# A decode attention block: two opening loads moved ahead of the start barrier

## The chip, the cores and the metric

One core of one Trainium2 chip (trn2). The metric is the device time of the whole program in microseconds, lower is better. The span in a profile runs from the first recorded instruction to the last, and is shorter than the time of the same run.

## The reference, cut to what matters

One decoding step for four sequences: layernorm, attention over a cache of 8192 positions, and a small gated MLP branch on the same input.

```python
def reference(A_x, A_k_cache, A_v_cache, A_wq, A_wo, B_x, B_w1, B_w2, B_w3, B_w4):
    # B=4, D=448, Hq=16, Hkv=8, Sk=8192, Dh=256, F=1792; all bf16
    x = A_x
    xn = _layernorm(x, axis=-1)
    s = _A_ref(xn, A_k_cache, A_v_cache, A_wq, A_wo)      # q = xn@wq; softmax(q k^T) v; @wo
    g = _silu(_B_ref(xn, B_w1, B_w2, B_w3, B_w4))         # only w3, w4 matter for Sq=1
    return x + s * g
```

K and V are 4 x 8 heads of 4 MiB each: 64 loads of 4 MiB, 268 of the 279 MB that the kernel reads.

## The kernel before

SyncE's program issues every large load in the order in which the stream is to run. ScalarE issues one small one, x (4 rows of 896 bytes). `begin_ahead` takes these first loads out of their programs and puts them behind the Drain with which their engine arrives at the program's opening barrier.

```python
def begin_ahead(nc, loads):
    # ... takes the loads out of their blocks ...
    first = blocks[0].instructions
    for load in reversed(loads):
        at = next(n for n, i in enumerate(first)
                  if i.engine == load.engine and isinstance(i, mybir.InstDrain))
        first.insert(at + 1, load)
```

```python
        def prog_sp(sp):
            ahead.append(sp.sem_inc(S["pause"], 1))          # two steps that let x go first
            ahead.append(take(sp, "pause"))
            ahead.append(sp.dma_start(vflat[1][:, 0:DK * HDH], ... A_wq ...).then_inc(S["dwq"], 16))
            sp.dma_start(... B_w3 ...).then_inc(S["dw3"], 16)
            sp.dma_start(... B_w4 ...).then_inc(S["dw4"], 16)

            def load_k(h):
                b, g = where(h)
                if h >= 2:
                    sp.wait_ge(S["v_k"], h - 1)              # buffer of head h-2 free
                sp.dma_start(kn_dst(h), A_k_cache[b, g]...).then_inc(S["dk%d" % (h % 2)], 16)
            # ... load_v waits for v_v in the same way ...
            load_k(0)
            load_k(1)
            load_wo(NLATE, HQ, "dwo")                        # 2688 KB
            for h in range(2, NH):
                load_k(h)
                load_v(h - 2)
            load_v(NH - 2)
            load_v(NH - 1)
            # ... LATE pieces of wo, 448 and two times 224 KB, then the store ...
```

```python
        def prog_act(act):
            ahead.append(act.dma_start(x_sb[:, :], x2d).then_inc(S["dx"], 16))
            # ...
        def prog_dve(v):
            # ...
            c(v.memset(q_ps[:, 0:QW], 0.0))
            v.wait_ge(S["dx"], 16)
            c(v.tensor_copy(x_f[:, :], x_sb[:, :]))          # "the cast": the front chain begins
            # ... layernorms, then with PE: q, h, gelu, h2, the gate ...
            # ... per head: evacuations of the K transposes, then
                    v.sem_inc(S["v_k"], 1)                   # lets SyncE issue K of head h+2
        def prog_pe(pe, xn_mark, xn2_mark):
            # ... front chain: transposes, q, h, h2, hs ...
            for i in range(NWARM):                           # NWARM = 14 warming matmuls
                pe.matmul(psv[0:PVW, 0:QW], pT[:, 0, 0:PVW], wq_sb[:, 0, 0:QW], start=True, stop=True)
            # ... then per head: f_t, 128 transposes of K in 16 groups, waits for the K load ...
```

The K buffer has two slots. So the third K load, called K2 below, is the first load that waits for computed work: for VectorE's last evacuation of head 0, which needs the whole front chain and the warming matmuls done.

## Time and profile before

| | before |
|---|---|
| median of the runs, us | 653.56 (653.2 to 653.56, 3 runs) |
| profiled run, us / its span, us | 653.45 / 652.0 |
| first wq packet, us into the span | 1.26 |
| last wo piece landed, us into the span | 649.13 |
| tail from there to the end, us | 2.87 |
| outside the span, us | 1.45 |

The prediction below shows and reads the page, the stretches and the opening. Two things are added here. First the start of head 0 on PE (timeline of the kernel before: start us, length us, engine, line, operation; L596 are the warming matmuls, L604 the transposes of K):

```profile
23.94 5.26 PE L596 MATMUL psv<-vb,pT 128*32 128x512 bf16 x14
30.07 1.05 PE L604 MATMUL pst<-ident_b,kn 128*128 128x128 bf16 x16 [0.87 <-PEq L278]
```

Second SyncE's issue of K2, from its timeline:

```profile
41.77 0.33 SPq L237 DMA_DIRECT2D kn<-in_A_k_cache_dram  x1
```

The load ahead of K2 in the stream is the large piece of wo; its 16 engines land it between 44.35 and 46.24.

### The profile page before, as it was taken

How to read it: one execution, taken by the hardware profiler on the slowest of the kernel's cores; microseconds unless marked ns; L12 is line 12 of the kernel's file. 1: busy time of each engine (PE TensorE's matmuls, PEld its weight loads, DVE VectorE, ACT ScalarE, POOL GpSimd, SP SyncE). 2: the span in 40 equal slices, each digit the busy share in tenths (PEclk: the TensorE clock that was granted, in tenths of full speed). 3: DMA queues.
4: the chain of work that ended last, by engine and by line, in shares of the span. 5: the costliest groups of instructions: out<-in, count | busy, mean ns of one | idle time of the engine just before them, and what ended most of it. 6: DMA issues, size and time to landing. Idle time of an engine off the chain costs nothing. (4 is left out here: it accounts for less than half of the span.)

```text
span 652.0 us, 22813 instructions
## 1 busy us (share of the span) xinstructions
PE 550.5 (84%) x9937; PEld 470.7 (72%) x9937; DVE 276.9 (42%) x622; ACT 255.8 (39%) x364; POOL 3.6 (1%) x17
## 2 busy tenths in 40 slices
PE   2799997988887987888897888898888798878897
PEld 1487876987676876667787766787677688757774
DVE  7344544343343443434443444444344344434442
ACT  4144543443343443323443333444234344423440
POOL 2000000000000000000000000000000000000000
PEclk9998999888799898889987888988779987978999
DMA  9999999999999999999999999999999999999997
GB/s 374 440 420 433 430 434 434 430 438 426 440 426 440 426 440 426 440 428 436 432 435 430 434 434 426 440 426 440 426 440 428 438 428 438 430 436 430 434 429 301
DMA packets 12353, 279.13 MB, mean 428 GB/s; under 512 B 1204, under 2 KB 3256, under 8 KB 3768
## 3 DMA queue, kind: packets, MB, share of 16 engines
q1 hardware_dynamic: 12328, 278.99, 99.5%
q8 instruction: 7, 0.11, 0.1%
q10 hardware_dynamic: 16, 0.01, 0.0%
q14 instruction: 2, 0.02, 0.0%
HBM read 278.99 MB, written 0.00 MB: 428 GB/s over the span
## 5 line engine op out<-in xcount | busy, mean ns | idle before, releaser
L604 PE MATMUL pst<-ident_b,kn 128*128 128x128 bf16 x4096 | 342.7, 237 | 81.4 <-PEq L278 79.3
L309 ACT ACTIVATE kT<-pst 128x1024 bf16<-128x1024 bf16 x224 | 229.3, 1024 | 357.5 <-ACTq L278 356.3
L604 PEld LDWEIGHTS pst<-ident_b,kn 128*128 128x128 bf16 x4096 | 271.7, 107 | 87.2 <-issue 86.6
L307 DVE COPY kT<-pst 128x1024 bf16<-128x1024 bf16 x288 | 197.5, 691 | 261.1 <-DVEq L278 261.1
L616 PE MATMUL psc<-qc,kT 128*128 128x2 bf16 x4096 | 178.2, 164 | 0.0
L616 PEld LDWEIGHTS psc<-qc,kT 128*128 128x128 bf16 x4096 | 157.1, 98 | 28.7 <-issue 28.5
L655 PE MATMUL psv<-vb,pT 128*4 128x512 bf16 x1056 | 85.6, 378 | 0.0
L634 PE MATMUL psm<-sel,po 128*128 128x2 f32 x272 | 36.8, 257 | 0.5 <-PEq L278 0.5
L634 PEld LDWEIGHTS psm<-sel,po 128*128 128x128 f32 x272 | 34.8, 196 | 0.9 <-issue 0.9
L655 PEld LDWEIGHTS psv<-vb,pT 128*4 128x4 bf16 x1056 | 21.8, 82 | 15.0 <-issue 0.4
L466 DVE TENSOR_REDUCE rmax<-psc 128x2 f32<-128x128 f32 x32 | 9.3, 292 | 48.1 <-DVEq L278 48.1
L484 DVE COPY po<-psv 128x512 f32<-128x512 f32 x34 | 23.5, 691 | 4.0 <-DVEq L278 3.3
L331 ACT ACTIVATE pT<-psc,negb 128x64 bf16<-128x64 f32 x66 | 20.6, 332 | 5.4 <-ACTq L278 5.4
L471 DVE TENSOR_REDUCE gmax<-psm 2x1 f32<-2x128 f32 x32 | 8.9, 279 | 32.3 <-DVEq L278 32.3
L628 PEld LDWEIGHTS psm<-diag,ones_f 2*128 2x128 f32 x66 | 13.5, 253 | 6.3 <-issue 5.0
L628 PE MATMUL psm<-diag,ones_f 2*128 2x2 f32 x66 | 16.2, 313 | 1.1 <-PEq L278 0.9
L331 ACT ACTIVATION_READ_ACCUMULATOR pT<-psc,negb 128x1 f32 x66 | 13.6, 206 | 0.0
L624 PEld LDWEIGHTS psm<-ident_f,rmax 128*2 128x2 f32 x32 | 2.6, 80 | 14.0 <-issue 14.0
L646 PE MATMUL psm<-rowsum,ones_f 128*128 128x2 f32 x64 | 11.6, 251 | 0.0
L552 PE MATMUL pst<-ident_b,xn_b 4*128 4x4 bf16 x14 | 0.6, 161 | 11.5 <-DVE xn_b L379 6.8
L646 PEld LDWEIGHTS psm<-rowsum,ones_f 128*128 128x128 f32 x64 | 9.5, 188 | 0.0
L474 DVE TENSOR_SCALAR diag<-ident_f,gmax 2x2 f32<-2x2 f32 x32 | 6.9, 217 | 4.8 <-DVEq L278 1.1
(101 smaller groups left out, 101.1 us busy)
## 6 DMA issues: line engine op xcount, KB each, us to landing
kn<-in_A_k_cache_dram SPq DMA_DIRECT2D x32, 4096.0 KB, 25.5
vb<-in_A_v_cache_dram SPq DMA_DIRECT2D x31, 4096.0 KB, 30.5
vb<-in_A_wq_dram SPq DMA_DIRECT2D x1, 3584.0 KB, 11.4
vb<-in_B_w_dram SPq DMA_DIRECT2D x2, 1568.0 KB, 16.3
wo_sb<-in_A_wo_dram SPq DMA_DIRECT2D x1, 2688.0 KB, 43.3
kn<-in_A_v_cache_dram SPq DMA_DIRECT2D x1, 2048.0 KB, 24.7
kn<-in_A_v_cache_dram SPq DMA_DIRECT2D x1, 1024.0 KB, 26.7
kn<-in_A_v_cache_dram SPq DMA_DIRECT2D x2, 512.0 KB, 27.9
```

Of the source, the lines that this page charges most:

```text
L307: engine.tensor_copy(dst, src).then_inc(S["v_ev"], 1)
L309: engine.activation(dst, src, ACT.Copy).then_inc(S["a_ev"], 1)
L331: ins = act.activation(pv_p[:, :, hh], sc[:, :, hh], ACT.Exp, bias=negb[:, s, hh:hh + 1], scale=SCALE, accum_out=rowsum[:, s, hh:hh + 1])
L466: v.tensor_reduce(rmax[:, :], psc[h % 2][:, 0:NCH * REP].rearrange("p (k h) -> p h k", h=REP), AX.X, ALU.max).then_inc(S["v_rmax"], 1)
L471: v.tensor_reduce(gmax[:, :], psm[0:REP, 0:P], AX.X, ALU.max).then_inc(S["v_s"], 1)
L484: v.tensor_copy(po[:, slot], psv[:, 0:CP * DH]).then_inc(S["v_po"], 1)
L604: ins = pe.transpose(dst[:, t * P:(t + 1) * P], kn[:, h % 2, GC * j + kl, half * P:(half + 1) * P], ident_b[:, :])
L616: ins = pe.matmul(psc[h % 2][:, kk * REP:(kk + 1) * REP], kT[:, j % RING, t * P:(t + 1) * P], qc[:, h % 2, half, :], start=(half == 0), st ...
L628: pe.matmul(psm[:, P:P + REP], ones_f[0:REP, :], diag[:, :], start=True, stop=True).then_inc(S["p_m2"], 1)
L634: ins = pe.matmul(dst(dh)[:, 0:width], po[:, slot, i * DH + dh:(i + 1) * DH:NHALF], sel[:, i, 0:width], start=(i == 0), stop=(i == CP - 1))
L646: pe.matmul(psm[:, P + REP:P + 2 * REP], ones_f[:, :], rowsum[:, h % 2, :], start=True, stop=True)
L655: ins = pe.matmul(psv[o:o + CP * REP, 0:CP * DH], pT[:, h % 2, kk * REP:(kk + CP) * REP], src[:, kk:kk + CP, :].rearrange("p c d -> p (c d)"),
```

## The change

The intent: start the stream earlier. wq is to be the first thing that SyncE does, ahead of its arrival at the barrier, and the two pause steps that kept x first are dropped; in exchange x is to go ahead of ScalarE's arrival.

```diff
-    first = blocks[0].instructions
-    for load in reversed(loads):
-        at = next(n for n, i in enumerate(first)
-                  if i.engine == load.engine and isinstance(i, mybir.InstDrain))
-        first.insert(at + 1, load)
+    first = list(blocks[0].instructions)
+    for n, load in enumerate(loads):
+        own = [i for i in first if i.engine == load.engine]
+        drain = next(i for i in own if isinstance(i, mybir.InstDrain))
+        if n == 0:
+            later = own[0:2]
+            first = [i for i in first if i not in later]
+            at = first.index(drain)
+            first[at:at] = later
+            at = first.index(later[0])
+        else:
+            at = first.index(drain)
+        first.insert(at, load)
     blocks[0].instructions = first
 ...
         def prog_sp(sp):
-            ahead.append(sp.sem_inc(S["pause"], 1))
-            ahead.append(take(sp, "pause"))
-            ahead.append(sp.dma_start(
+            ahead.insert(1, sp.dma_start(
                 vflat[1][:, 0:DK * HDH], ... A_wq ...).then_inc(S["dwq"], 16))
 ...
         def prog_act(act):
-            ahead.append(act.dma_start(x_sb[:, :], x2d).then_inc(S["dx"], 16))
+            ahead.insert(0, act.dma_start(x_sb[:, :], x2d).then_inc(S["dx"], 16))
```

Loop bodies, tiles, loads and their order are the same.

More of the change, by code (lines that the diff above doesn't have):

```diff
@@ L182, in bass_recurrent_scan__gqa_block_cached__mixer_s_mlp__decode_kernel @@
         S = {n: es.enter_context(nc.semaphore(n)) for n in (
-            ["dx", "dwq", "dw3", "dw4", "dwo", "dk0", "dk1", "dv0", "dv1", "dout", "pause"]
+            ["dx", "dwq", "dw3", "dw4", "dwo", "dk0", "dk1", "dv0", "dv1", "dout"]
             + ["dvl%d" % i for i in range(NPIECE)] + ["dwl%d" % i for i in range(len(LATE))]
```

## The prediction

> **What bounds the kernel now.** I read the page first: busy shares, the 40 slices, the DMA queues, the chain that ended last. Then the landings of the loads, the queue's own waits, and last the first 12 us as a timeline, because the change touches nothing else. From the page:
>
> ```profile
> span 652.0 us, 22813 instructions
> ...
> PE 550.5 (84%) x9937; PEld 470.7 (72%) x9937; DVE 276.9 (42%) x622; ACT 255.8 (39%) x364; POOL 3.6 (1%) x17
> ...
> DMA  9999999999999999999999999999999999999997
> GB/s 374 440 420 433 430 434 434 430 438 426 440 426 440 426 440 426 440 428 436 432 435 430 434 434 426 440 426 440 426 440 428 438 428 438 430 436 430 434 429 301
> ...
> q1 hardware_dynamic: 12328, 278.99, 99.5%
> ```
>
> The reader is to see one queue, SyncE's, that keeps the 16 DMA engines busy 99.5% of the span and moves 278.99 MB. No slice but the first and the last falls under 420 GB/s. PE at 84% has slack. The kernel is one unbroken stream of loads with a lead-in and a tail. The same cut by stretches (us, then busy time of PE, PEld, DVE, ACT and POOL, granted clock, DMA share, GB/s):
>
> ```profile
> 0.00:0.50 0.50, 0.00 (x0) 0.00 (x0) 0.00 (x0) 0.00 (x0) 0.20 (x4) 1.00 0.00 0
> 0.50:1.00 0.50, 0.00 (x0) 0.00 (x0) 0.08 (x1) 0.11 (x1) 0.27 (x2) 1.00 0.00 0
> ...
> 44.35:645.00 600.65, 517.66 (x9454) 447.91 (x9448) 251.74 (x536) 239.49 (x345) 0.00 (x0) 0.90 1.00 433
> ...
> 649.13:652.00 2.87, 0.55 (x8) 0.23 (x4) 0.77 (x2) 0.00 (x0) 0.00 (x0) 1.00 0.01 4
> ```
>
> Nothing moves in the first microsecond; then the stream runs at 433 GB/s; the last piece of wo lands at 649.13 and 2.87 us of output work follow. Packets in flight, counted from the trace's packet records, stay near the 16 engines from 1.55 us to 647 us without a hole. So
>
> time = start of the first wq packet (1.26 us) + stream (to 649.13) + tail (2.87) + 1.5 outside the span (653.45 for the profiled run less 652.0).
>
> Only something that shifts the first term, or tears a hole into the second, moves the result. The opening, from the timeline (start us, length us, engine, line):
>
> ```profile
> 0.21 0.56 ACTq L312 DMA_DIRECT2D x_sb<-in_A_x_dram  x1
> ...
> 0.24 0.41 SPq L222 DMA_DIRECT2D vb<-in_A_wq_dram  x1
> ...
> 0.73 0.20 POOL L284 MEMSET ident_f<- 128x128 f32 x1 [0.29 <-POOLq L816]
> 0.78 0.34 SPq L226 DMA_DIRECT2D vb<-in_B_w_dram  x1
> ...
> 0.92 0.48 DVE L383 MEMSET pst<- 128x512 f32 x1 [0.92 <-ACTq L816]
> ...
> 2.01 0.38 DVE L385 CAST x_f<-x_sb 4x448 f32<-4x448 bf16 x1 [0.60 <-DMA x_sb<-in_A_x_dram]
> ```
>
> Both loads leave 0.2 us into the span already, before the barrier opens. What lies ahead of wq is in the trace's records of SyncE, which the views leave out as not busy: Drain (its arrival at the barrier) at 0.000, the pause increment at 0.069, the pause wait at 0.149, wq at 0.237. ScalarE has its Drain at 0.133 and x at 0.207. TensorE arrives last, at 0.322; GpSimd sees the fourth arrival at 0.532, opens at 0.610, and SyncE passes at 0.695.
>
> **What the Trainium skill says.** "DMA: Bandwidth & Descriptors", Where 436 GB/s comes from, puts the ceiling of the fabric at 435.2 GB/s. The trace agrees: 433 GB/s over 600 us, and each 4 MiB load lands 9.68 us after the one before (4194304 B / 9.68 us = 433 GB/s). So no packing helps; only the start can. The same page, Issuing engines are not separate DMA queues, says loads issued from different engines run on the same 16 DMA engines. "Perfetto Trace Analysis", DMA Instruction — HWDGE, says that an issue locks a shared descriptor generator for exclusive use; before's x and wq issues overlap (0.21 to 0.77, 0.24 to 0.65), which neither shows nor refutes it. "DMA: Bandwidth & Descriptors", Queues, rings and completion order, says each DMA engine takes turns between its rings at packet granularity. Before's x packets start at 1.156 to 1.610 and wq's from 1.257 on, so x was mostly first and the trace does not show a small load queued behind wq.
>
> **The change, part by part.**
>
> 1. Pause steps gone, and wq ahead of SyncE's Drain. The three SyncE steps ahead of wq took 0.237 us together. wq becomes the first instruction of SyncE's program, so its issue moves from 0.237 to about 0.00. Issue to first packet took 1.257 - 0.237 = 1.02 us; at the same delay the first packet starts near 1.02. All of it lies on the path that sets the end: -0.24 us.
>
> 2. x ahead of ScalarE's Drain. The built program no longer contains the opening register moves among which the change places x; the load simply comes first, at ScalarE's own start, 0.133 instead of 0.207: -0.07 us. x feeds the layernorm chain, not the stream: 0 on the path.
>
> 3. The barrier opens later, since two of its arrivals now stand behind an issue. SyncE arrives near 0.41 (length of the wq issue), ScalarE near 0.133 + 0.563 = 0.70 plus a step, 0.74, against TensorE's 0.322 before. From last arrival to release before: 0.610 - 0.322 = 0.29, of which GpSimd's own Drain (to 0.49) covered a part; so the release comes near 0.74 + 0.13 = 0.87, some 0.26 us later than 0.610. That puts SyncE's w3 issue near 1.03 instead of 0.78 and VectorE's first memset near 1.18 instead of 0.92. The w3 load only has to be queued before wq's first engine is through, at 10.71: 9 us to spare, 0 on the path. The memset ends near 1.67, ahead of x's landing near 1.9: 0 on the chain.
>
> 4. Nothing else moves: loop bodies, loads and their order are the same, 75 DMA issues on SyncE in both builds.
>
> Sum: -0.24 + 0 + 0 = -0.24 us. 653.56 - 0.24 = 653.3 us.
>
> **The rivals.**
>
> A. x gets caught behind wq. Before, x was issued 0.03 us ahead of wq; now SyncE starts 0.133 us before ScalarE, so wq goes first by about that much. x is four rows on four of the 16 engines. If there it has to wait for one wq descriptor, that is 1.6 to 2.4 us (what the first 28 KB packets took), and x lands near 3.2 instead of 2.0. I hold this more likely than not, 60%. It delays the whole front chain (layernorm, q, gelu) by about 1.3 us. Does it reach the stream? Ahead of the compute lie wq, w3, w4, k0, k1 and wo, issued without a wait; their last landings are 44.35 (first engine) to 46.24 (last engine). The load after them waits for VectorE's work on head 0, and is issued at 41.77. Allowing the 1.02 us from issue to packet, the slowest engine has 46.24 - 41.77 - 1.02 = 3.4 us of slack. Moreover PE starts head 0 at 30.07, just after k0's landing at 29.94, and ahead of it are 14 warming matmuls (23.94 to 29.2), so 0.9 us of the delay vanish there. The next tight place is the K load at 60.26, with the V load before it landing from 63.71 to 65.69: 65.69 - 60.26 - 1.02 = 4.4 us. A 1.3 us delay is swallowed: still 653.3.
>
> B. x waits for all of wq on its engines. If a packet held a whole engine's share of wq, x would land near 10.5, 8.5 us late; less the slack of 3.4 + 0.9, a hole of some 4 us: 657.5. Against it: the packet records show wq's descriptors one at a time, each 1.06 us, so turns every descriptor are possible. Chance 5%.
>
> C. Nothing is gained, because wq's first packet is held by something other than its issue (the 1.02 us grows), or because the engine that ends last is another one. The engines end 2.14 us apart at 646.99 and 649.13, and the spread grew from 0.95 (w4) to 2.05 (k0) about when instruction fetches cut in at 27.9. That is luck of the run of a few tenths, and the three runs of before differ by 0.36 themselves: 653.0 to 653.8. Chance some 25%.
>
> D. A big win. Would need the steady part to be waiting for something in the opening; 99.5% busy speaks against it.
>
> **Range and chances.** 653.3, with the run-to-run step of 0.36 us on either side and a bit for rival C: 652.7 to 653.8 holds it 8 times in 10. Two per cent is 13 us; the whole lead-in is 1.26 us, so faster by 2% is out of reach: 0.3%. Slower by 2% would need x to come 17 us late: 0.7%. Within 2%: 99%.
>
> **What would show each step right or wrong.** Step 1: SyncE's wq issue stands at 0.00 and its landing shifts from 11.63 to about 11.4 with it; the last landing goes from 649.13 to about 648.9 and the span from 652.0 to 651.8. Step 2 and rival A: VectorE's first cast starts at 1.9 if x was in time, near 3.2 if it was caught. Step 3: w3's issue near 1.03, the first memset of VectorE near 1.18. Rival B: the cast near 10, a queue that runs dry at 46. I am wrong if the DMA row shows a slice under 9 in the middle, or if the span moves by more than 0.6 us.

## The result, and the profile after

| | before | after |
|---|---|---|
| median of 4 runs each, us | 653.52 (653.2 to 653.56) | 654.91 (654.25 to 655.51) |
| profiled run / span, us | 653.45 / 652.0 | 655.51 / 653.7 |
| mean granted clock | 0.908 | 0.906 |
| VectorE's cast of x starts, us | 2.01 | 4.78 |
| K2 issued, us | 41.77 | 43.14 |
| last wo piece landed, us | 649.13 | 650.03 |
| tail, us | 2.87 | 3.62 |
| outside the span, us | 1.45 | 1.85 |

The ratio is 1.0022, with a 95% interval of 1.0005 to 1.0039. A ratio here is the mean time of one kernel's fast runs over that of the other's fast runs of the same rounds, so it is not quite the ratio of the medians. So the time stayed within 2%, as expected, but it went up by 1.4 us where 0.24 us were to be won; the prediction had 652.7 to 653.8. The last row holds 0.40 us of that; the account below is first of what happens within the span.

The page of the changed kernel still shows one saturated queue:

```profile
span 653.7 us, 22811 instructions
...
DMA  9999999999999999999999999999999999999996
GB/s 380 446 403 417 440 425 441 425 441 425 427 439 427 439 427 439 427 439 429 437 428 437 429 437 429 437 429 437 431 435 433 433 433 433 433 433 435 431 426 284
...
q1 hardware_dynamic: 12328, 278.99, 99.4%
```

The first slice moves more (380 GB/s instead of 374): the stream does start earlier. The third moves less: 403 instead of 420. Each slice is 16.3 us, so the third covers 32.7 to 49.0. The DMA row shows 9 there and hides it; the GB/s row does not. 17 GB/s over 16.3 us are 0.28 MB, at 433 GB/s some 0.6 us of lost transfer.

The opening, by the timeline of the changed kernel:

```profile
0.00 0.41 SPq L228 DMA_DIRECT2D vb<-in_A_wq_dram  x1
...
0.12 0.57 ACTq L318 DMA_DIRECT2D x_sb<-in_A_x_dram  x1
...
1.10 0.20 POOL L290 MEMSET ident_f<- 128x128 f32 x1 [0.67 <-POOLq L822]
...
1.11 0.33 SPq L232 DMA_DIRECT2D vb<-in_B_w_dram  x1
...
1.29 0.48 DVE L389 MEMSET pst<- 128x512 f32 x1 [1.29 <-PEq L822]
...
4.78 0.38 DVE L391 CAST x_f<-x_sb 4x448 f32<-4x448 bf16 x1 [3.01 <-DMA x_sb<-in_A_x_dram]
```

wq is issued at 0.00, and x 0.12 us behind it instead of 0.03 us ahead. The barrier opens 0.37 us later (the release in the records is at 0.980, before at 0.610). And the cast waits 3.01 us for x: it starts at 4.78, not at 2.01.

The packet records tell why so long. Times in us, of the four engines that carry one row of x each:

```
                         before                       after
first wq packet          1.257                        1.032
x data packets start     1.156  1.179  1.205  1.610   2.815  3.067  3.106  3.332
x completion (4 bytes)   1.215  1.262  1.593  1.645   4.187  4.221  4.247  4.445
```

On each of these engines the row of x waits for wq's first 28 KB descriptor (1.5 to 2.4 us long), and then the 4-byte write that tells the semaphore waits for a second one. The small load pays two turns, not one. The four late increments of x's semaphore come at 4.52 to 4.75.

What this does to PE, by its timeline for the changed kernel:

```profile
26.23 5.46 PE L602 MATMUL psv<-vb,pT 128*32 128x512 bf16 x14
31.61 1.07 PE L610 MATMUL pst<-ident_b,kn 128*128 128x128 bf16 x16
```

Of the 2.77 us by which x is late, 2.29 reach the warming matmuls (23.94 to 26.23) and 1.54 reach head 0 (30.07 to 31.61); the rest lies under waits that were there before. SyncE's issue of K2 then comes 1.37 us later:

```profile
43.14 0.33 SPq L243 DMA_DIRECT2D kn<-in_A_k_cache_dram  x1
```

The stream shows what follows. Stretches (us, then busy time of PE, PEld, DVE, ACT and POOL, clock, DMA share, GB/s), first of before, then of after:

```profile
45.00:46.00 1.00, 1.00 (x17) 0.84 (x15) 0.55 (x3) 0.00 (x0) 0.00 (x0) 1.00 1.08 453
615.00:625.00 10.00, 8.23 (x157) 7.33 (x147) 4.92 (x11) 4.57 (x8) 0.00 (x0) 1.00 0.99 426
649.00:653.00 4.00, 0.68 (x11) 0.33 (x7) 0.77 (x2) 0.00 (x0) 0.00 (x0) 0.97 0.01 3
```

```profile
45.00:46.00 1.00, 1.00 (x23) 0.40 (x19) 0.37 (x2) 0.00 (x0) 0.00 (x0) 1.00 0.55 229
615.00:625.00 10.00, 7.00 (x85) 6.18 (x78) 3.33 (x7) 2.64 (x6) 0.00 (x0) 0.66 0.97 419
649.00:653.00 4.00, 2.35 (x45) 1.97 (x44) 0.93 (x3) 0.00 (x0) 0.00 (x0) 1.00 0.04 16
```

In the microsecond from 45 to 46 the stream moves 229 GB/s where before moved 453: this is the hole. The other two stretches belong to the tail. From 617.9 to 624.7 the profiled run of the changed kernel was granted half the clock, in the last head (clock 0.66 over the stretch), and PE still had 45 instructions to do after 649 instead of 11; counted from each kernel's own last landing it is 24 against 8. In before the last such window fell at 598 to 605, ahead of the last head.

To measure the hole: the K loads of a running stream land 9.68 us apart, and from the mean landing (over the 16 engines) of the wo piece to that of K2 it is 9.88 us when nothing is missing. What lies over 9.88 is called the hole below. The "lead" is the first engine's landing of wo less the issue of K2.

```
mean landing, us       wo      K2      gap     hole    first landing of wo   K2 issue   lead
before                44.99   54.88    9.89    0.01    44.35                 41.77      2.58
after                 44.75   55.25   10.50    0.62    44.24                 43.14      1.10
```

The packet records split it. In before the 20 descriptors of K2 that start first, of 32 KB each, take 1.21 us: they were queued while the engines still worked. In after the 13 that start first, on 13 engines, take 1.28 to 2.17 us. Their excess over 1.21, summed and divided by 16 engines, is 0.40 us; the other 0.2 us or so of the hole is idle time before them. A real stop is not needed for the slow descriptors: in the third profile of the changed kernel (below) several engines went on to K2 some 6 ns after wo's completion write, the idle time is only 0.04 us above that of before, and still 10 of the first descriptors took 1.29 to 1.90 us. They start 1.28 to 2.2 us after K2's issue; in before the first starts 2.25 us after it. Why a freshly issued load starts slowly was not tested.

So the mean landings shift, after less before, by -0.23 to -0.34 us from wq to wo (wo itself -0.24), then +0.37 at K2, +0.56 at K3 (a second small hole of 0.19), and +0.92 by the 19th load. From there to the end the shift stays. The slow growth from 0.56 to 0.92 lies in packets that took a little longer between 115 and 170 us; it is seen in this profile alone and was not explained.

### The profile page after: what moved, and what is told of

It is laid out like the page before. It is cut to its first block, busy times and chain, and to the rows that moved or that the text cites. A ratio compares the mean times of both kernels' runs of the same rounds, so it can differ in the third digit from the quotient of the medians.

```text
span 653.7 us, 22811 instructions
## 1 busy us (share of the span) xinstructions
PE 550.5 (84%) x9937; PEld 471.5 (72%) x9937; DVE 276.9 (42%) x622; ACT 255.7 (39%) x364; POOL 3.6 (1%) x17
```

## The experiments

All eleven runs gave correct results. Each set shares its runs of the kernel before. "Last wo" is the landing of the last piece, in the profiled run.

### The changed kernel again

No edit. Its second set of runs, to see how firm the loss is.

> The changed kernel once more, on the same chip as the next three. Theory X (x caught behind wq, the third K load issued too late, a hole in the stream): 654.3 to 655.5 us, VectorE's first cast near 4.8, third K load issued near 43.1, its mean landing 10.5 us after wo's instead of 9.9. Theory B (the later opening of the barrier costs it): the same time. Theory L (luck of this one set of runs, such as where the half-clock windows fell): back to 653.3 to 653.6.

Measured: 654.29 us (654.18 to 655.09) against 653.72 (9 runs), ratio 1.0011, interval 0.9997 to 1.0024. Cast at 4.47, K2 at 42.92, hole 0.50, last wo 649.51. The hole is there again, a bit smaller, since x waited 0.3 us less; the loss of time is about half the first one.

### x alone ahead of the barrier

The changed kernel with SyncE's part undone.

```diff
-            at = first.index(drain)
+            at = first.index(drain) + n      # pause steps and wq are n = 1, 2, 3: behind the Drain, as before
...
+            ahead.append(sp.sem_inc(S["pause"], 1))
+            ahead.append(take(sp, "pause"))
```

> The ScalarE half of the change alone: x ahead of ScalarE's barrier arrival, wq behind the pause steps as before. The barrier then opens as late as in the changed kernel (x's issue of 0.57 us stands before the arrival), but x goes out 0.12 us ahead of wq. Theory X: cast at 1.9 to 2.1, third K load near 41.7, time as before, 653.3 to 653.6. Theory B: the barrier is still 0.37 us late, so 654 or more.

Measured: 653.38 us (653.34 to 654.57), ratio 1.0000 (0.9986 to 1.0013). The timeline, opening and K2's issue:

```profile
0.12 0.56 ACTq L320 DMA_DIRECT2D x_sb<-in_A_x_dram  x1
...
1.29 0.48 DVE L391 MEMSET pst<- 128x512 f32 x1 [1.29 <-PEq L824]
...
1.69 0.37 DVE L393 CAST x_f<-x_sb 4x448 f32<-4x448 bf16 x1
...
41.72 0.33 SPq L245 DMA_DIRECT2D kn<-in_A_k_cache_dram  x1
```

The barrier opens as late as in the changed kernel (release at 0.986, VectorE's first memset at 1.29), yet the cast starts at 1.69, K2 is issued at 41.72, and the hole is 0.01. The late barrier alone costs nothing at K2. At K3 there is a hole of 0.10 here too, though x was in time; "Put together" comes back to it.

### wq alone ahead of the barrier

The changed kernel with ScalarE's part undone.

```diff
         if n == 0:
-            later = own[0:2]
-            ...
-            at = first.index(later[0])
+            at = first.index(drain) + 1      # x behind its Drain, as before
```

> The SyncE half alone: wq first in SyncE's program without pause steps, x behind ScalarE's barrier arrival as before. The barrier opens only 0.1 us or so later than before (SyncE arrives near 0.46 instead of TensorE's 0.32). wq leads x by 0.2 us. Theory X: cast near 4.8, third K load near 43, time 654.3 to 655.5 like the changed kernel. Theory B: barrier nearly on time, so 653.3 to 653.6.

Measured: 654.36 us (653.74 to 654.78), ratio 1.0008 (0.9995 to 1.0022). The timeline:

```profile
0.00 0.41 SPq L224 DMA_DIRECT2D vb<-in_A_wq_dram  x1
...
0.20 0.57 ACTq L314 DMA_DIRECT2D x_sb<-in_A_x_dram  x1
...
0.99 0.48 DVE L385 MEMSET pst<- 128x512 f32 x1 [0.99 <-ACTq L818]
...
4.52 0.38 DVE L387 CAST x_f<-x_sb 4x448 f32<-4x448 bf16 x1 [3.04 <-DMA x_sb<-in_A_x_dram]
...
42.95 0.33 SPq L239 DMA_DIRECT2D kn<-in_A_k_cache_dram  x1
```

Here the barrier is nearly on time (memset at 0.99, before 0.92), but x is behind wq, and everything else follows as in the changed kernel: cast at 4.52, K2 at 42.95, hole 0.50, another 0.25 at K3, last wo 649.87. Together with the run before it this puts the hole at K2 on the order of x and wq, not on the barrier.

### Both ahead of the barrier, order kept

The changed kernel with the two pause steps put back ahead of wq.

```diff
+            ahead.append(sp.sem_inc(S["pause"], 1))
+            ahead.append(take(sp, "pause"))
-            ahead.insert(1, sp.dma_start(
+            ahead.append(sp.dma_start(
```

> Both loads ahead of their engine's barrier arrival as in the change, but the two pause steps kept in front of wq, so that x leads wq by about 0.04 us. Barrier as late as in the changed kernel, wq's issue near 0.16 instead of 0.24. Theory X: cast near 2.0, third K load near 41.8, stream 0.08 us early, time 653.1 to 653.6. Theory B: 654 or more.

Measured: 653.65 us (653.44 to 653.97), ratio 0.9999 (0.9985 to 1.0013).

```profile
0.13 0.56 ACTq L320 DMA_DIRECT2D x_sb<-in_A_x_dram  x1
...
0.17 0.41 SPq L230 DMA_DIRECT2D vb<-in_A_wq_dram  x1
```

x leaves 0.04 us ahead of wq, the cast starts at 1.76, K2 at 41.68, no hole; the stream runs 0.09 us ahead of before's. The hole is gone with the late barrier still in place.

### The changed kernel with fewer warming matmuls

```diff
-    NWARM = 14
+    NWARM = 6
```

> The changed kernel with 6 instead of 14 warming matmuls ahead of head 0. x stays caught behind wq (cast near 4.5), but PE is free some 3 us earlier, so head 0 can start on k0's landing near 29.5 to 30 instead of 31.6. Theory X: third K load issued near 41.0 to 41.6, no hole (its mean landing 9.9 us after wo's), and the 0.24 us at the start is kept: 653.1 to 653.6. If the late x did its harm in another way, for instance through the late q or the barrier, the time stays at 654.3.

Measured: 653.94 us (653.44 to 655.31) against 653.66 (11 runs), ratio 1.0008 (0.9995 to 1.0021). The cast is as late as ever (4.73), but head 0 no longer is:

```profile
28.95 1.86 PE L610 MATMUL pst<-ident_b,kn 128*128 128x128 bf16 x16 [0.20 <-PEq L284]
```

It starts at 28.95, and though its first 16 transposes run at half clock (1.86 us instead of 1.07), K2 is issued at 41.79. Hole 0.00; the stream stays 0.21 us ahead of before's right to the end, and last wo is 648.74, 0.39 earlier than before. So a late x costs the stream nothing as long as K2 is issued in time, and the 0.24 us that the change was made for are real there. The time, above what was expected, does not show them: 0.40 us more lie outside the span than in before, and the tail scatters (both under "Put together").

### The kernel before with more warming matmuls

`NWARM = 18` in the kernel before: delay head 0 with x in time.

> The kernel before with 18 instead of 14 warming matmuls: x in time, barrier in time, wq as before, but head 0 starts later by up to 1.5 us. Theory X: third K load issued near 43, the hole of 0.5 to 0.6 us appears here as well: 654.0 to 654.8. If only the opening itself matters, 653.3 to 653.8.

Measured: 654.01 us (653.31 to 655.85), ratio 1.0005 (0.9992 to 1.0018). A miss: I expected K2 near 43, but four more matmuls moved head 0 only to 30.91, K2 to 42.42, and the stream of that run was 0.37 us late from the landing of wq on. The lead is 2.45 us and there is no hole. So it says nothing against the mechanism, but it did not test it.

### The kernel before with fewer warming matmuls

`NWARM = 6` in the kernel before, meant as a control for the one above.

> The kernel before with 6 warming matmuls, as a control for the first of this call: theory X says that head 0 already starts within 0.2 us of k0's landing (30.07 against 29.94), so third K load at 41.5 to 41.8 and the same time as before, 653.3 to 653.7. If fewer warming matmuls are worth something by themselves, this gains as much as the first of this call does.

Measured: 655.27 us (654.62 to 655.6), ratio 1.0021 (1.0008 to 1.0034). I expected no change. PE's timeline, SyncE's issue of K2, and two stretches:

```profile
29.95 1.86 PE L604 MATMUL pst<-ident_b,kn 128*128 128x128 bf16 x16 [3.46 <-PEq L278]
```

```profile
44.19 0.33 SPq L237 DMA_DIRECT2D kn<-in_A_k_cache_dram  x1
```

```profile
30.00:35.00 5.00, 5.00 (x50) 4.79 (x51) 1.45 (x3) 1.76 (x2) 0.00 (x0) 0.50 0.97 419
44.00:45.00 1.00, 1.00 (x22) 0.51 (x19) 0.81 (x2) 0.00 (x0) 0.00 (x0) 1.00 0.58 222
```

PE was idle for 3.46 us ahead of head 0 and then ran at half clock (0.50 from 30 to 35), which the Trainium skill, "TensorE: Matmul & The Clock Gate", Part 1: The HAM clock gate, describes: the default is throttled, and an idle window of about 3.4 us brings it back. K2 was issued at 44.19, a lead of 0.36 us, and the stream has a hole of 1.39 us (222 GB/s from 44 to 45). This miss is the best control of all: x was in time, the barrier was in time, nothing of the change was in the kernel, and still the same loss came by the same route, 1.47 us in the last landing of wo (650.60 against 649.13).

### The changed kernel with wq in two pieces

Let x in sooner: wq first as 128 runs of 4 KB, then as 128 runs of 24 KB.

```diff
+            for lo, hi in ((0, HDH), (HDH, DK * HDH)):
+                ahead.append(sp.dma_start(vflat[1][:, lo:hi], wq_src[:, lo:hi]).then_inc(S["dwq"], 16))
...
-            take(pe, "dwq", 16)
+            take(pe, "dwq", 32)
```

> The changed kernel with wq loaded in two pieces: first one row in seven (128 runs of 4 KB), then the rest (128 runs of 24 KB). x still goes out after wq. If x is held for one wq descriptor ahead of its data and a second ahead of its completion write, then with 4 KB descriptors the cast starts near 2.0 to 2.6 instead of 4.5, the third K load goes out near 41.5 and the time is 653.1 to 653.6. If x waits for wq's whole share on its engines or for the generator of descriptors, the cast stays near 4.5 or gets later, and the time stays at 654.3.

Measured: 653.55 us (653.44 to 654.2), ratio 0.9996 (0.9983 to 1.0009).

```profile
0.00 0.88 SPq L231 DMA_DIRECT2D vb<-in_A_wq_dram  x2
...
0.12 0.57 ACTq L319 DMA_DIRECT2D x_sb<-in_A_x_dram  x1
...
2.93 0.38 DVE L392 CAST x_f<-x_sb 4x448 f32<-4x448 bf16 x1 [0.98 <-DMA x_sb<-in_A_x_dram]
```

x is still behind wq, but its data now goes at 1.73 to 2.38 and its completion at 2.09 to 2.58. The cast at 2.93 is a little later than the 2.0 to 2.6 expected, K2 goes at 41.69, hole 0.02, last wo 648.85 (0.28 earlier than before). Both turns shrink with the descriptor size: this confirms what x was waiting for. It is the best of the changed family, and by the times not distinguishable from the kernel before: its spans are 0.63 us shorter on average (651.76 against 652.39 in the same rounds), but 0.47 us of that are lost outside the span (1.92 against 1.45).

### More load queued ahead of K2

The changed kernel with the late pieces of wo (896 KB) issued right behind the large one, so that K2 has about 2 us more room.

> The changed kernel with the three last pieces of wo (0.9 MB, 2.1 us of the stream) moved from the end of SyncE's program to behind the first piece of wo. x stays caught (cast near 4.5) and the third K load is still issued near 43, but the first engine now runs out 2.1 us later, so the lead grows from 1.1 to about 3.2 us. Theory X: no hole at the third K load (under 0.05 us); the last V landing, mean over engines, comes 0.2 to 0.3 us before that of the kernel before plus 2.1 us. The tail gets longer, since PE's last work then waits for V instead of wo: 654.5 to 656. If the late front chain costs stream time in another way than through this lead, the hole of 0.5 to 0.6 us stays.

Measured, 3 rounds: 656.57 us (655.76 to 656.86) against 653.8 (9 runs), ratio 1.0036 (1.0021 to 1.0052). x is caught (cast 4.39), K2 goes at 42.12, 4.36 us ahead of the first landing of the last wo piece, and the hole is gone. It costs elsewhere, as expected though a bit more: the last V pieces now end the stream, so its last piece lands at 647.79 instead of 645.81 on average and all its work stands behind it.

### The two-piece wq with one wo piece less at the end

The kernel with wq in two pieces, and `LATE = ((0, 1), (2,))`: 224 KB more ahead of K2.

> A candidate for better than both: wq first and split as in the last experiment, and one 224 KB piece of wo moved from the end to the front, which gives the third K load 0.5 us more lead (about 3.2) and the fourth as well. Stream 0.15 to 0.3 us earlier than before, no hole; the end has 0.5 us less of wo to hide the last V's work behind, of which 0.4 us was spare. 653.0 to 653.6; with a half-clock window in the last head up to 654.4. If the spare was needed, 653.6 to 654.

Measured, 5 rounds: 654.01 us (653.78 to 655.11), ratio 1.0004 (0.9991 to 1.0018). A miss as a try for the better version: lead 2.88, no hole, last wo 648.74, but no gain in time.

### The changed kernel a third time

> The changed kernel a third time, for the size of the loss and to see what of it repeats. Theory X: cast 4.4 to 4.8, third K load 42.9 to 43.2, hole 0.5 to 0.65 us in this profile too. The end of the stream 0.2 to 0.4 us later than before's unless the fourth K load is late as well, the rest of the difference from the tail: 2.8 to 2.9 us without and 3.2 to 3.7 us with a half-clock window inside the last head. 654.0 to 655.2.

Measured, 5 rounds: 654.18 us (653.73 to 655.1), ratio 1.0005 (0.9992 to 1.0019). Cast 4.74, K2 at 42.50, lead 1.62, hole 0.23, last wo 649.00. x was as late as the first time, but the 14 warming matmuls took 4.87 us instead of 5.46, so K2 came earlier and the hole is smaller than expected. The mean landings at the end are 0.05 us ahead of before's: in this profile the stream lost nothing in all.

### Put together

Lead of K2 against the hole, over the profiles in which the large wo piece is what lies ahead of K2:

```
                                lead    hole
before                          2.58    0.01
x alone ahead                   2.67    0.01
wq in two pieces                2.64    0.02
order kept                      2.63    0.01
after, 6 warming matmuls        2.48    0.00
before, 18 warming matmuls      2.45    0.00
two pieces, one late wo less    2.88    0.00
after, third time               1.62    0.23
after, second time              1.25    0.50
wq alone ahead                  1.22    0.50
after, first time               1.10    0.62
before, 6 warming matmuls       0.36    1.39
```

From 2.45 us up there is no hole; below 1.7 every us of lead that is missing costs about one of stream. A line through the lower rows is near hole = 1.8 - lead. Between 1.62 and 2.45 there is no run. The times alone would not carry this: of the runs with a hole of 0.5 us or less none has an interval that excludes equality. The landings do.

K3's lead is another matter. It was 2.17 to 2.32 us in three profiles, with a hole at K3 of 0.10 (x alone), 0.25 (wq alone) and 0.19 (after, first time), and these are the three in which the clock was halved for 6.83 us from 54.4 to 54.7 on, in head 1. In the other ten such a window is absent there or half as long, K3's lead is 3.09 us or more, and the hole at most 0.03. The three are of both kinds, x early and x late, so this second hole goes by the clock and not by x, as far as profiles tell; no experiment tried it.

The tail is a second, independent part. Sorted by whether a window of half clock of 6.8 us began between 616 and 620, in the last head:

```
such a window:    after 3.62, after again 3.73, third time 3.52, two pieces 3.43, order kept 3.25, 18 warming 3.25
none or half one: before 2.87, x alone 2.86, wq alone 2.86, after with 6 warming 2.86, before with 6 warming 2.85,
                  two pieces and one late wo less 3.06
```

It falls on kernels of both kinds, with and without the change. On the six profiles with the window the tail is 0.4 to 0.9 us longer. (More load ahead of K2 has it too, but ends on V and is left out.) That this is the cause of the longer tail was read from profiles, not tried by an experiment. Over all its runs the kernel before took 653.2 to 654.88 us, a scatter that is somewhat wider still.

The third part lies outside the span, and it is the one that every single run shows. Time less span, from the lists of runs:

```
wq first, no pause steps:   1.81 to 1.96 in 37 of 38 runs, 2.40 in one
    (after, three sets; wq alone; after with 6 warming; two pieces; two pieces and one late wo less; more load ahead of K2)
pause steps kept:           1.39 to 1.50 in all 51 runs
    (before; x alone; order kept; before with 18 and with 6 warming)
```

So SyncE's half of the change, with the pause steps dropped, costs about 0.40 us that the span does not hold, more than the 0.24 us that it wins; ScalarE's half does not (x alone), and wq ahead of the barrier with the pause steps kept does not either (order kept). The traces show one thing beside it: the last 8 KB packet of the instruction queue starts 1.07 to 1.19 us after the last instruction in the profiles of the first row, and -0.05 to +0.23 us in the others; the one run with 2.40 has a further packet at 2.08. Whether that fetch is the cause was not tested, nor which of the two, the missing steps or wq in the first place, brings it.

## Why the prediction was right or wrong

**Step 1, the earlier stream: right.** The first wq packet came at 1.03 (said: 1.02), and the landings from wq to wo moved by -0.23 to -0.34 us, wo's by -0.24 (said: -0.24). What it won in the stream was lost again outside the span, as told above. In the runs without a hole, those with 6 warming matmuls and with wq in two pieces, last wo is 0.39 and 0.28 earlier than in before.

**Step 2, x a little earlier: wrong as far as x's landing goes.** The issue did move, to 0.116 instead of 0.207, but x was caught behind wq. The prediction itself gave that 60% as rival A, while its sum went on with a cast near 1.9 as one of two outcomes. (Its "1.6 to 2.4 us" for the first 28 KB packets leaves some out: the first 16 of before took 1.26 to 2.45.)

**Step 3, the barrier: right in kind.** It opened 0.37 us later, said 0.26. The two kernels with a late barrier and x first show that this costs nothing at K2.

**Rival A is what happened, and the step of it that failed is "swallowed".** It was mis-sized in two terms. The first is the wait for x: "one wq descriptor", x near 3.2, against 4.47 to 4.78 measured. The completion write needs a turn of its own. The second is the slack of K2, put at 46.24 - 41.77 - 1.02 = 3.4 us; the runs show 2.58 - 1.8, about 0.8 us. The 46.24 is the last engine's landing, but K2 has to be there for the first engines, which land from 44.35 on and are through with their data 0.33 us before that (the first completion write of before's wo is at 44.02). And the stream does not just lose the time until the next packet: the first descriptors of the late load took 1.28 to 2.17 us instead of 1.21. A delay of 1.37 us against 0.8 us of slack leaves a hole of 0.57 us by this sum; 0.62 was measured. That is no independent check, since the 1.8 comes from a line through the same runs.

**The second step that failed is the last term of its sum, "1.5 outside the span",** taken as fixed, with "only something that shifts the first term, or tears a hole into the second, moves the result". That term went from 1.45 to 1.85 us with the change. Why is open; what is known is told under "Put together".

**Rival B did not happen.** x never waited for more than two descriptors per engine.

**Rival C's point on luck was right, but placed wrong.** Scatter that the few runs of before (0.36 us) did not show is, as far as the profiles tell, in the tail: a half-clock window in the last head. In the first profile of the changed kernel, which has one, the tail is 0.75 us longer.

**The sum for the profiled run:** -0.24 (earlier start) + 0.61 (hole at K2, by the shift of its landing from -0.24 to +0.37) + 0.19 (hole at K3) + 0.34 (the growth to the end that was not explained) = +0.90 in the last landing, and +0.75 in the tail: +1.66 in the span; with +0.40 outside it +2.06, which is 655.51 - 653.45.

**How large is the loss?** The means of the changed kernel lie 1.44, 0.75 and 0.42 us above those of the kernel before in the three sets. Only the first interval excludes equality. Some 0.4 us of each lie outside the span (1.82, 1.89 and 1.88 against 1.45), so that 1.07, 0.32 and -0.01 us are left within it (the first with 1.45 taken for before, whose other spans of that set are not on record). The stream's own balance, by the mean landings at the end against before's profile, is +0.92, +0.20 and -0.05 us in the three profiles. So the hole is shown in all three (0.62, 0.50, 0.23), but what repeats in the time is the part outside the span; the hole eats the earlier start, in two of the three profiles more than that, and the rest of the 1.44 is put down to the tail and to the growth that was not explained. The prediction missed on three counts: one mechanism undersized, one term taken as fixed, and the scatter of the tail not known from three runs.

**What stays open:** the slow growth between 115 and 170 us in the first profile, what makes up the 0.40 us outside the span, why a freshly issued load starts slowly, and why the hole at K3 opens at a longer lead than at K2. With V0 ahead of K3, a lead of 2.32 us gave 0.19, one of 2.21 gave 0.25 and one of 2.17 gave 0.10, while 3.24 gave 0.03.

**A version that beats both** was not found. The changed kernel with wq in two pieces keeps the earlier start without a hole, and its spans are shorter, but 0.47 us outside the span take nearly all of it back. A version that keeps its stream and avoids that was not tried.

## What to carry to other kernels

In a kernel that is one stream of loads, look for the first load that waits for computed work, and measure its lead by the first engine's landing of the load ahead of it, not the last one's; 2.45 us or more was enough at K2 here, 2.17 to 2.32 at K3 was not. A small load that the front chain waits for belongs ahead of the first large one, or the large one's first descriptors must be small: behind it, it paid two of its descriptors here. And look at the GB/s row, not only at the DMA tenths: a loss of half a microsecond shows as 420 against 403 in one slice and in no other row of the page. And set the time of the run beside the span: when the opening of a program is changed, what lies outside the span can change more than what was won within it.

## What the Trainium skill lacked or had wrong

- "DMA: Bandwidth & Descriptors", Queues, rings and completion order, gives the turn between queues as a packet of typically 9 to 17 descriptors. Here the turns came after every single 28 KB descriptor of wq (x's data at 2.82 to 3.33, after one descriptor of 1.5 to 2.4 us). wq has only 8 such descriptors per engine, so a turn of a whole packet would have held x until the end of wq, which landed from 10.59 on.
- The same page, Why a DMA increments its semaphore by 16 and not by 1, says that each engine's last descriptor writes the semaphore, and that the engines not used are counted at once; the trace agrees (x's semaphore moves first at 0.76, then four times at 4.52 to 4.75). It does not say that this write waits for a turn of its own when another queue is busy: 1.1 to 1.4 us more here (data at 2.82 to 3.33, completion at 4.19 to 4.45).
- No page says how early a load must be issued to follow a running stream without a hole. Here, at K2: none at a lead of 2.45 us or more from the first landing of the load ahead, about 1.8 less the lead below 1.7; and the first 32 KB descriptors of a load issued some 1 us before them took 1.28 to 2.17 us instead of 1.21.
- No page says that the time outside a profile's span can depend on how a program begins. Here: 1.39 to 1.50 us in 51 runs, 1.81 to 1.96 us in 37 of the 38 runs in which SyncE's program starts with a load.
